# K and V slabs of a decode attention on two DMA queues instead of one

## The chip, the cores and the metric

One core of one Trainium2 chip. The metric is the device time of one execution in microseconds (us); lower is better. The core has five engines: TensorE (PE, matrix products; its weight loads are PEld in the profile), VectorE (DVE), ScalarE (ACT), GpSimd (POOL) and SyncE (SP), which in this kernel only issues DMA transfers. Transfers run on 16 DMA engines that the queues of SP and ACT share.

## The reference

Two independent problems A and B, each one decode step of attention with a sliding window: 2 batches, 1 query row of 576 numbers, 32 query heads, 16 key/value heads of 128, and the last W = 4096 of 16384 cached positions. All in bf16.

```
q = (x @ wq)                                  # x [2,1,576], wq [576,4096]
k, v = k_cache[:, :, Sk-W:], v_cache[:, :, Sk-W:]   # each key/value head serves 2 query heads
p = softmax(q k^T * 128**-0.5)                # 4096 positions
out = (p v).reshape(2, 1, 4096) @ wo          # wo [4096,576]
return concatenate([out_A, out_B], axis=-1)   # [2,1,1152]
```

## The kernel before

**Pairs and slabs.** A "pair" is one batch and one key/value head of one problem: 32 pairs in A, 32 in B, NP = 64 in all, eight to a group G. Each pair needs one K slab and one V slab of 1 MB (128 partitions x 8 KB, 32 positions of 128 numbers in each partition). With wq (4.7 MB) and wo (4.7 MB) of both problems, 153 MB come in.

**Steps.** The program is written as a list of steps t (loop from line 662 on), each in four quarters q. An engine runs its instructions strictly in the order in which the loop adds them. In step t:

- X(t): VectorE transposes K slab t into `xt`, one instruction a quarter (line 679, 4 per slab; `xt` has 3 buffers). It waits for the slab's DMA.
- S(t-1): TensorE computes the scores of pair t-1 (line 700, 8 matmuls), into one PSUM bank for each group.
- PV(t-11): TensorE multiplies the weights of pair t-11 with its V slab (line 765, 8 matmuls; for the last seven pairs line 723, 32 small matmuls in four quarters). It waits for the slab's DMA. LAG = 11 is there because the softmax of a group needs all its eight pairs.
- For pairs up to 56, ScalarE (even pairs, line 780) or VectorE (odd, line 783) copies the result out of PSUM ("eviction"), and one step later TensorE adds it up with four small matmuls (line 743, "combine").
- Every second step: a normalization on VectorE (line 555), a clear (line 565) and the projection with `wo` on TensorE (line 582).
- After the eighth pair of a group, from step 8G+8 to 8G+10, its softmax: maximum (line 377), transposes and small matmuls on TensorE (lines 381, 406, 431, 451), bias copy and exponential on ScalarE (lines 419, 427), transposes and gather on VectorE (lines 473, 487).

So step t uses K slab t and V slab t-11. After the last K slab there are eleven steps that use V alone.

**The queue.** All slabs are loaded by SP, in one order (`stream`, lines 224 to 230): K0 ... K10, K11, V0, K12, V1, ... K63, V52, V53 ... V63. Slab number s of this list goes to slot s % 9 of `ring` (NR = 9 slots), and its DMA is issued when the last reader of slab s-9 is done: the fourth transpose for a K slab, the last PV matmul for a V slab (lines 249 to 273). The last slab, V63, is loaded in four quarters, each with a semaphore of its own. The weights stand in the same list, ahead of a K slab (`w_at`, lines 231 to 237, and `ensure_stream_until`, lines 298 to 309):

- wq of A, five transfers, before K0; wq of B, one transfer before each of K13 to K17.
- wo of group G before K slab min(63, 8G+6). From G = 2 on, its issue waits (line 291) until the last projection of group G-2 has freed the buffer, which comes in step 8G+4. SP issues in order, so what stands behind it waits too.

The issues of slabs are line 272 (line 264 for V63), of wq lines 281 and 282, of wo line 294. ScalarE issues only the two small loads of x at the start (line 220).

Of the kernel before, what the change touches and what calls it, by code (L numbers as in the profile page):

```python
# [58 lines left out]

def build_kernel(nc, probs, out, cfg=None):  # L60
    cfg = dict(cfg or {})
    NR = cfg.get("NR", 9)
    NKT = cfg.get("NKT", 3)
    NTB = cfg.get("NTB", 2)
    NZQ = 2
# [1 line left out]
    LAG = cfg.get("LAG", 11)  # L67
# [21 lines left out]
    NP = PP * NPROB  # L89
# [18 lines left out]
    def is_a(i):  # L108
        return i < NP - NB_TAIL
# [12 lines left out]
    with es:  # L122
        block = es.enter_context(nc.Block())
        sb = lambda name, shape, dt: es.enter_context(nc.sbuf_tensor(name, shape, dt))
        ring = sb("ring", [128, NR, SLABW], BF16)
# [37 lines left out]
        ring_sem = [sem("ring%d" % r) for r in range(NR)]  # L163
# [4 lines left out]
        lastq_sem = [sem("lastq%d" % q_) for q_ in range(4)]  # L168
# [4 lines left out]
        def dma_op(eng, sem_h, n_dmas, fn, deps, tag):  # L173
            op = S.add(eng, fn, deps, tag)
            dma_count[sem_h] = dma_count.get(sem_h, 0) + 16 * n_dmas
            op.dma = (sem_h, dma_count[sem_h])
            return op
# [43 lines left out]
            return last  # L221
        x_dma = dma_op("act", x_sem, NPROB, f_x, [], "xload")

        stream = []
        for t in range(NP + LAG):
            if t < NP:
                stream.append(("K", t))
            if t >= LAG:
                stream.append(("V", t - LAG))
        slab_idx = {key: s for s, key in enumerate(stream)}  # L230
        w_at = {}
        for P in range(NPROB):
            t0 = 0 if P == 0 else WQ_AT + 8 * GPP * (P - 1)
# [5 lines left out]
        slab_dma = {}  # L239
        slab_quarters = {}  # L240
        slab_last_reader = {}
# [4 lines left out]
        proj = {}  # L246
        next_stream = [0]

        def issue_slab(s):
            kind, i = stream[s]  # L250
            P, g, b = pair_info(i)
            src_t = probs[P][1] if kind == "K" else probs[P][2]
            src = src_t[b, g, Sk - W:Sk, :].rearrange("(p j) d -> p (j d)", p=128)
            r = s % NR
            deps = []
            if s >= NR:
                assert slab_last_reader.get(s - NR) is not None, ("ring too small / order", s)
                deps = [slab_last_reader[s - NR]]

            if s == len(stream) - 1 and kind == "V" and not is_a(i):  # L260
                qops = []
                for q_ in range(NQ):
                    def fq(e, r=r, src=src, q_=q_):
                        return e.dma_start(ring[:, r, q_ * TQ * 128:(q_ + 1) * TQ * 128],
                                           src[:, q_ * TQ * 128:(q_ + 1) * TQ * 128]).then_inc(lastq_sem[q_], 16)
                    qops.append(dma_op("sp", lastq_sem[q_], 1, fq, deps, "%s%d_q%d" % (kind, i, q_)))
                slab_dma[s] = qops[-1]
                slab_quarters[s] = qops
                return

            def f(e, r=r, src=src):
                return e.dma_start(ring[:, r, :], src).then_inc(ring_sem[r], 16)  # L272
            slab_dma[s] = dma_op("sp", ring_sem[r], 1, f, deps, "%s%d" % (kind, i))

        def issue_wq(P, ch):
            wqP = probs[P][3]
# [21 lines left out]
        def ensure_stream_until(s_needed):  # L298
            while next_stream[0] <= s_needed:
                s = next_stream[0]  # L300
                kind, i = stream[s]
                if kind == "K":
                    for wk, a_, b_ in w_at.get(i, []):
                        if wk == "wq":
                            issue_wq(a_, b_)
                        else:
                            issue_wo(a_)
                issue_slab(s)
                next_stream[0] += 1

        tbn = [0]
# [349 lines left out]

        NT = NP + LAG + 3
        for t in range(NT):
            for q in range(NQ):
                for fn in pe_pre.get((t, q), []):
                    fn()
# [2 lines left out]
                for fn in da_pre.get((t, q + 0.5), []):  # L669
                    fn()  # L670
                if t < NP:
                    sK = slab_idx[("K", t)]
                    ensure_stream_until(sK)
                    r = sK % NR
                    c = t % NKT
                    deps = [slab_dma[sK]]
                    if t >= NKT:
                        deps.append(Sop[(t - NKT, 2 * (q // 2) + 1)])
                    xop = S.add("dve", lambda e, r=r, c=c, q=q: e.transpose(  # L679
                        xt[:, c, q * 1024:(q + 1) * 1024].bitcast(FP32), ring[:, r, q * 1024:(q + 1) * 1024].bitcast(FP32)),  # L680
                        deps, "X_%d_%d" % (t, q))
                    EVop[(t, q)] = xop
                    if q == NQ - 1:
                        slab_last_reader[sK] = xop
                i = t - 1
                if 0 <= i < NP:
                    G = group_of(i)
# [16 lines left out]
                    deps = [EVop[(i, 2 * jh_)], EVop[(i, 2 * jh_ + 1)], qev[G], st_zero[G]]  # L704
                    Sop[(i, q)] = S.add("pe", fS, deps, "S_%d_%d" % (i, q))
                i = t - LAG
                if 0 <= i < NP and not is_a(i):
                    sV = slab_idx[("V", i)]
                    ensure_stream_until(sV)
                    r = sV % NR  # L710
                    G = group_of(i)
                    pr = G % NPT
                    pl = i % 8
                    k = i // 2
                    x = k % 2
                    P, g, b = pair_info(i)

                    def fPVb(e, r=r, pr=pr, pl=pl, x=x, b=b, q=q):
                        last = None
                        for jj in range(TQ):  # L720
                            j = q * TQ + jj
                            col = tile_cols(j) + 2 * pl
                            last = e.matmul(OT[x][:, b * 64:b * 64 + NS], ring[:, r, j * 128:(j + 1) * 128],  # L723
                                            pT[:, pr, col:col + NS], start=False, stop=True, skip_group_check=True)
                        return last
                    deps = [slab_quarters[sV][q] if sV in slab_quarters else slab_dma[sV], chain[(G, "pT")], ot_zero[k], ot_last_da[x]]
                    op = S.add("pe", fPVb, deps, "PVb_%d_%d" % (i, q))
                    PVop[(i, q)] = op
                    ot_last_pe[x] = op
                    if q == NQ - 1:  # L730
                        slab_last_reader[sV] = op
                if q == NQ - 1:
                    i = t - LAG - 1
                    if 0 <= i < NP and is_a(i):
# [11 lines left out]
                        deps = acc_ev[i] + [ot_zero[k], ot_last_da[x], p_ident_b]  # L746
# [3 lines left out]
                        ot_last_pe[x] = op  # L750
                    i = t - LAG
                    if 0 <= i < NP and is_a(i):
                        sV = slab_idx[("V", i)]
                        ensure_stream_until(sV)
                        r = sV % NR
                        G = group_of(i)
                        pr = G % NPT

                        def fPV(e, r=r, pr=pr, pl=i % 8, i=i):
                            last = None  # L760
                            n_ = 0
                            for cb in range(4):
                                for jh in range(2):
                                    j0_ = 16 * jh + 4 * cb
                                    last = e.matmul(ACC[i % 2][0:8, 0:512], pC[:, pr, jh, pl, 8 * cb:8 * cb + 8],  # L765
                                                    ring[:, r, j0_ * 128:(j0_ + 4) * 128],
                                                    start=(n_ == 0), stop=(n_ == 7))
                                    n_ += 1
                            return last
                        deps = [slab_dma[sV], chain[(G, "pC")]]  # L770
                        if i >= 2:
                            deps += acc_ev[i - 2]
                        op = S.add("pe", fPV, deps, "PV_%d" % i)
                        PVop[(i, 0)] = op
                        slab_last_reader[sV] = op
                        d = [op]
                        if i >= 2:
                            d.append(comb[i - 2])
                        if i % 2 == 0:
                            ev_ = S.add("act", lambda e, i=i: e.activation(acc_sb[0:8, i % 2, :], ACC[i % 2][0:8, :], ACTF.Copy),  # L780
                                        d, "accev_%d" % i)
                        else:
                            ev_ = S.add("dve", lambda e, i=i: e.tensor_copy(acc_sb[0:8, i % 2, :], ACC[i % 2][0:8, :]),  # L783
                                        d, "accev_%d" % i)
                        evs = [ev_]
                        acc_ev[i] = evs

                for fn in da_post.get((t, q), []):
                    fn()
# [99 lines left out]
```

## Time and profile before

| what | us |
|---|---|
| median of 3 runs | 377.95 (376.51 to 378.59) |
| the profiled execution's own time | 378.42 |
| its span in the profile | 376.6 |
| TensorE busy | 296.3 (79%) |
| VectorE busy | 211.7 (56%) |
| ScalarE busy | 36.9 (10%) |
| X, one transpose (line 679) | 0.673, 256 times |
| S, one matmul (line 700) | 0.391, 512 times |
| PV, one matmul (line 765) | 0.397, 456 times |
| a slab, median from issue to landing | 19 to 20 |

The span is what the profiler saw from the first to the last instruction; the execution's own time is 1.8 us longer. "L679" in a profile line is line 679 of the code. In lists of groups and in timelines, a bracket at the end of a line tells how long the engine stood idle before it and what ended that. "SPq" and "ACTq" are the issues of DMA on those engines. A line of waits reads: engine and line, what it waited for, us in total, how many times, the longest.

### The profile page before, as it was taken

Reading aid. Unit: us, or ns where it says so; the run is one execution under the profiler, and the core shown is the slowest. Engines: PE = TensorE matmul, PEld = TensorE weight load, DVE = VectorE, ACT = ScalarE, POOL = GpSimd, SP = SyncE. Lnnn points to the kernel's source line nnn. Section 1 sums busy time; section 2 is a strip of 40 time slices with the busy share of each in tenths; the row PEclk is TensorE's granted clock in tenths of the full one; section 3 lists DMA queues with packets and bytes.
Section 4 is the critical chain, followed back from the end, with each engine's and each line's share of the span. In section 5 each row is a group of like instructions: output and inputs, shape, how many; then the busy total and the mean of one; then the engine's idle time right before and its main releaser. Section 6 shows DMA issues by size and latency. Waiting matters only on the chain.

```text
span 376.6 us, 4709 instructions
## 1 busy us (share of the span) xinstructions
PE 296.3 (79%) x1960; PEld 118.6 (31%) x1960; DVE 211.7 (56%) x429; ACT 36.9 (10%) x105; POOL 6.7 (2%) x22
## 2 busy tenths in 40 slices
PE   0397778375898989969897789868799689959786
PEld 0243223122334433313332233323333233313245
DVE  3196894235664567626864567636773467633311
ACT  1101101000101010100101010100101001000100
POOL 7000000000000000000000000000000000000000
PEclk9999989799999999989999899999999899998899
DMA  8999999999999999999999999999999999999991
GB/s 310 425 421 412 419 419 411 422 420 422 422 416 417 418 420 420 410 421 421 423 419 411 422 419 422 410 422 421 422 422 410 420 425 419 413 421 418 425 411 70
DMA packets 28661, 153.41 MB, mean 407 GB/s; under 512 B 2392, under 2 KB 10592, under 8 KB 11360
## 3 DMA queue, kind: packets, MB, share of 16 engines
q1 hardware_dynamic: 28632, 153.11, 98.9%
q8 instruction: 15, 0.25, 0.3%
q14 instruction: 6, 0.05, 0.0%
q10 hardware_dynamic: 8, 0.00, 0.0%
HBM read 153.10 MB, written 0.00 MB: 407 GB/s over the span
## 4 chain that ended last, share of the span: by engine, by line
DMA 44%; PE 33%; DVE 10%; SPq 9%; issue 1%; ACT 1%
DMA ring<-in_B_v_cache_dram 17%; DMA ring<-in_A_v_cache_dram 15%; PE acc L765 15%; PE st L700 11%; DMA ring<-in_A_k_cache_dram 8%; SPq L272 7%; DMA ring<-in_B_k_cache_dram 5%; DVE xt L679 4%; PE ot L582 3%; DVE acc_sb L783 2%; PE ot L723 2%; PE ot L743 1%; ACT pR L427 1%; DVE m L377 1%; DVE pT L473 1%
## 5 line engine op out<-in xcount | busy, mean ns | idle before, releaser
L679 DVE STREAM_TRANSPOSE xt<-ring 128x512 f32<-128x512 f32 x256 | 159.3, 673 | 66.0 <-DMA ring<-in_A_k_cache_dram 38.5
L765 PE MATMUL acc<-ring,pC 128*8 128x512 bf16 x456 | 114.7, 397 | 38.1 <-DMA ring<-in_A_v_cache_dram 22.9
L700 PE MATMUL st<-xt,zq 128*128 128x512 bf16 x512 | 134.7, 391 | 4.9 <-DVE xt L679 4.5
L700 PEld LDWEIGHTS st<-xt,zq 128*128 128x128 bf16 x512 | 42.7, 98 | 74.1 <-issue 28.5
L765 PEld LDWEIGHTS acc<-ring,pC 128*8 128x8 bf16 x456 | 36.0, 89 | 91.1 <-DMA ring<-in_A_v_cache_dram 24.5
L783 DVE CAST acc_sb<-acc 8x512 bf16<-8x512 f32 x28 | 19.0, 679 | 66.8 <-PE acc L765 66.8
L780 ACT ACTIVATE acc_sb<-acc 8x512 bf16<-8x512 f32 x29 | 17.0, 586 | 186.1 <-PE acc L765 186.1
L582 PE MATMUL ot<-wob,oTn 128*2 128x288 bf16 x128 | 20.8, 285 | 3.5 <-DVE ot L565 3.2
L743 PEld LDWEIGHTS ot<-ident_b,acc_sb 8*128 8x128 bf16 x228 | 9.2, 92 | 24.1 <-issue 16.1
L743 PE MATMUL ot<-ident_b,acc_sb 8*128 8x56 bf16 x228 | 15.6, 185 | 0.8 <-DVE acc_sb L783 0.8
L509 PE MATMUL tb<-xT,wqb 128*128 128x56 bf16 x256 | 10.2, 192 | 6.4 <-DMA wqr<-in_A_wq_dram 6.4
L582 PEld LDWEIGHTS ot<-wob,oTn 128*2 128x2 bf16 x128 | 8.0, 82 | 15.5 <-issue 8.1
L509 PEld LDWEIGHTS tb<-xT,wqb 128*128 128x128 bf16 x256 | 9.8, 99 | 7.9 <-DMA wqr<-in_A_wq_dram 6.5
L381 PE MATMUL tb<-ident_f,m 128*1 128x128 f32 x8 | 2.2, 270 | 11.7 <-DVE m L377 11.7
L555 DVE TENSOR_TENSOR oTn<-ot,rsb 128x4 bf16<-128x4 f32 x32 | 4.1, 127 | 11.2 <-PE ot L723 7.4
L541 ACT ACTIVATE zq<-tb 32x64 bf16<-32x64 f32 x32 | 7.1, 221 | 31.9 <-PE tb L523 31.6
L509 PE MATMUL tb<-xT,wqr 128*128 128x56 bf16 x64 | 9.5, 192 | 0.0
L473 DVE STREAM_TRANSPOSE pT<-pR 128x512 bf16<-128x512 bf16 x8 | 5.7, 711 | 4.6 <-ACT pR L427 4.6
L419 ACT ACTIVATE bias_sb<-tb 128x1 f32<-128x1 f32 x8 | 1.4, 171 | 61.0 <-PE tb L406 61.0
L723 PE MATMUL ot<-pT,ring 128*128 128x56 bf16 x224 | 7.0, 187 | 0.4 <-issue 0.4
L723 PEld LDWEIGHTS ot<-pT,ring 128*128 128x128 bf16 x224 | 6.2, 96 | 2.0 <-issue 1.9
L565 DVE MEMSET ot<- 128x128 f32 x30 | 5.0, 165 | 3.1
(50 smaller groups left out, 71.9 us busy)
## 6 DMA issues: line engine op xcount, KB each, us to landing
ring<-in_A_k_cache_dram SPq DMA_DIRECT2D x32, 1024.0 KB, 20.2
ring<-in_A_v_cache_dram SPq DMA_DIRECT2D x32, 1024.0 KB, 19.8
ring<-in_B_k_cache_dram SPq DMA_DIRECT2D x32, 1024.0 KB, 20.3
ring<-in_B_v_cache_dram SPq DMA_DIRECT2D x31, 1024.0 KB, 19.3
wob<-in_A_wo_dram SPq DMA_DIRECT2D x4, 1152.0 KB, 18.4
wob<-in_B_wo_dram SPq DMA_DIRECT2D x4, 1152.0 KB, 9.5
wqb<-in_A_wq_dram SPq DMA_DIRECT2D x4, 1024.0 KB, 8.0
wqb<-in_B_wq_dram SPq DMA_DIRECT2D x4, 1024.0 KB, 21.9
```

The costliest lines, as they stand in the source:

```text
L272: return e.dma_start(ring[:, r, :], src).then_inc(ring_sem[r], 16)
L473: chain[(G, "pT")] = S.add("dve", lambda e: e.transpose(pT[:, pr, 0:PW], pR[:, G % 2, :]), deps, "cTpx_%d" % G)
L509: last = e.matmul(bank[:, hl * 64:hl * 64 + NS], w_, x_, start=(ch == 0), stop=(ch == NCH - 1))
L541: last = e.activation(dst, src, ACTF.Copy)
L582: last = e.matmul(OT[half][0:Bb, ACC0:ACC0 + NH], oTn[:, orr, h, :], wob[:, pc, hsl + h, half * NH:(half + 1) * NH], start=False, stop=Tru ...
L679: xop = S.add("dve", lambda e, r=r, c=c, q=q: e.transpose(xt[:, c, q * 1024:(q + 1) * 1024].bitcast(FP32), ring[:, r, q * 1024:(q + 1) * 1 ...
L700: last = e.matmul(ST[x][:, 0:512], zq[:, p4, zr, pl, 16 - 16 * jh:144 - 16 * jh], mv, start=False, stop=True, skip_group_check=True)
L723: last = e.matmul(OT[x][:, b * 64:b * 64 + NS], ring[:, r, j * 128:(j + 1) * 128], pT[:, pr, col:col + NS], start=False, stop=True, skip_g ...
L743: last = e.matmul(OT[x][:, b * 64:b * 64 + NS], acc_sb[0:8, i % 2, 128 * jl4:128 * jl4 + 128], ident_b[0:8, 2 * jl4:2 * jl4 + NS], start=F ...
L765: last = e.matmul(ACC[i % 2][0:8, 0:512], pC[:, pr, jh, pl, 8 * cb:8 * cb + 8], ring[:, r, j0_ * 128:(j0_ + 4) * 128], start=(n_ == 0), st ...
L780: ev_ = S.add("act", lambda e, i=i: e.activation(acc_sb[0:8, i % 2, :], ACC[i % 2][0:8, :], ACTF.Copy), d, "accev_%d" % i)
L783: ev_ = S.add("dve", lambda e, i=i: e.tensor_copy(acc_sb[0:8, i % 2, :], ACC[i % 2][0:8, :]), d, "accev_%d" % i)
```

## The change

The nine slots are divided: 4 for SP's queue, 5 for ScalarE's.

- SP's list is now K0 to K63 with the weights ahead of them as before, and at its end V56, V58, V60 and V62. Entry n goes to slot n % 4 and waits for the last reader of entry n-4.
- The other 60 V slabs (V0 to V55, V57, V59, V61, V63) are issued by ScalarE, in this order, into five slots of their own. The issue of V slab number n of this list is added to ScalarE's instructions right behind the point where the last reader of number n-5 was added (for pairs with an eviction, behind the eviction), and waits for that reader. The first five, V0 to V4, are issued after the last transpose of K6 to K10.
- V63 is still loaded in four quarters, now by ScalarE.

Nothing else changes: the steps, the order of all other instructions and the bytes that are moved are the same. The core of the diff:

```
-    NR = cfg.get("NR", 9)
+    NRK = cfg.get("NRK", 4)
+    NRV = cfg.get("NRV", 5)
+    NR = NRK + NRV
...
-        stream = []
-        for t in range(NP + LAG):
-            if t < NP:
-                stream.append(("K", t))
-            if t >= LAG:
-                stream.append(("V", t - LAG))
-        slab_idx = {key: s for s, key in enumerate(stream)}
+        V_LATE = NP - 8
+        sp_v = [i for i in range(V_LATE, NP) if i % 2 == 0]
+        act_v = [i for i in range(NP) if i not in sp_v]
+        stream = [("K", t) for t in range(NP)] + [("V", i) for i in sp_v]
+        k_slot = {key: n % NRK for n, key in enumerate(stream)}
+        v_slot = {("V", i): NRK + n % NRV for n, i in enumerate(act_v)}
+        slot_of = dict(k_slot)
+        slot_of.update(v_slot)
...
-        def issue_slab(s):
-            kind, i = stream[s]
+        def issue_slab(eng, key, deps):
+            kind, i = key
...
-            slab_dma[s] = dma_op("sp", ring_sem[r], 1, f, deps, "%s%d" % (kind, i))
+            slab_dma[key] = dma_op(eng, ring_sem[r], 1, f, deps, "%s%d" % (kind, i))
+
+        next_act = [0]
+
+        def act_issue_after(op_key, op):
+            n = next_act[0]
+            if n >= len(act_v):
+                return
+            want = ("K", LAG - NRV + n) if n < NRV else ("V", act_v[n - NRV])
+            if op_key == want:
+                issue_slab("act", ("V", act_v[n]), [op])
+                next_act[0] += 1
...
-                issue_slab(s)
+                issue_slab("sp", stream[s], [slab_last_reader[stream[s - NRK]]] if s >= NRK else [])
...
         for t in range(NT):
+            if t == NP:
+                ensure_stream_until(len(stream) - 1)
...
                     if q == NQ - 1:
                         slab_last_reader[sK] = xop
+                        act_issue_after(sK, xop)
...
                     if q == NQ - 1:
                         slab_last_reader[sV] = op
+                        act_issue_after(sV, op)
...
                         acc_ev[i] = evs
+                        act_issue_after(sV, op)
```

More of the change, by code (lines that the diff above doesn't have):

```diff
@@ L253, in issue_slab @@
             src = src_t[b, g, Sk - W:Sk, :].rearrange("(p j) d -> p (j d)", p=128)
[L254 to L260, printed above, removed]
+            r = slot_of[key]
+            if key == ("V", NP - 1):
                 qops = []
@@ L265, in fq @@
                                            src[:, q_ * TQ * 128:(q_ + 1) * TQ * 128]).then_inc(lastq_sem[q_], 16)
-                    qops.append(dma_op("sp", lastq_sem[q_], 1, fq, deps, "%s%d_q%d" % (kind, i, q_)))
-                slab_dma[s] = qops[-1]
-                slab_quarters[s] = qops
+                    qops.append(dma_op(eng, lastq_sem[q_], 1, fq, deps, "%s%d_q%d" % (kind, i, q_)))
+                slab_dma[key] = qops[-1]
+                slab_quarters[key] = qops
                 return
@@ L671, in build_kernel @@
                 if t < NP:
-                    sK = slab_idx[("K", t)]
-                    ensure_stream_until(sK)
-                    r = sK % NR
+                    sK = ("K", t)
+                    ensure_stream_until(t)
+                    r = slot_of[sK]
                     c = t % NKT
@@ L707, in build_kernel @@
                 if 0 <= i < NP and not is_a(i):
-                    sV = slab_idx[("V", i)]
-                    ensure_stream_until(sV)
-                    r = sV % NR
+                    sV = ("V", i)
+                    r = slot_of[sV]
                     G = group_of(i)
@@ L752, in build_kernel @@
                     if 0 <= i < NP and is_a(i):
-                        sV = slab_idx[("V", i)]
-                        ensure_stream_until(sV)
-                        r = sV % NR
+                        sV = ("V", i)
+                        r = slot_of[sV]
                         G = group_of(i)
```

## The prediction

> **What bounds the kernel now.** I read the page first, then the waits, then the timeline of the start and of the last 40 us. The page's slices show the DMA engines full in all slices but the last, and one queue carries nearly all of it:
>
> ```profile
> DMA  8999999999999999999999999999999999999991
> GB/s 310 425 421 412 419 419 411 422 420 422 422 416 417 418 420 420 410 421 421 423 419 411 422 419 422 410 422 421 422 422 410 420 425 419 413 421 418 425 411 70
> q1 hardware_dynamic: 28632, 153.11, 98.9%
> ```
>
> So the stream of 153.1 MB is the limit, not an engine. The completions in the trace, transfer by transfer, say how even it is: K63 lands at 340.98 us, V61 ten slabs later at 365.81, so one 1 MB slab costs **2.483 us**. A change of queues removes no byte. What it can change is whether the engines ever run dry, their rate, and **the order** in which slabs arrive.
>
> Order matters only where compute cannot absorb it, so the next view is TensorE's timeline at the end (start, us, line, form):
>
> ```profile
> 338.54 2.40 PE L765 MATMUL acc<-ring,pC 128*8 128x512 bf16 x8 [3.32 <-DMA ring<-in_B_v_cache_dram]
> 340.87 3.03 PE L700 MATMUL st<-xt,zq 128*128 128x512 bf16 x8
> ...
> 344.04 1.89 PE L765 MATMUL acc<-ring,pC 128*8 128x512 bf16 x8
> ...
> 346.98 1.48 PE L700 MATMUL st<-xt,zq 128*128 128x512 bf16 x6
> 348.39 0.28 PE L743 MATMUL ot<-ident_b,acc_sb 8*128 8x56 bf16 x4
> 348.60 1.89 PE L765 MATMUL acc<-ring,pC 128*8 128x512 bf16 x8
> 351.86 0.27 PE L381 MATMUL tb<-ident_f,m 128*1 128x128 f32 x1 [1.37 <-DVE m L377]
> ...
> 372.02 1.62 PE L723 MATMUL ot<-pT,ring 128*128 128x56 bf16 x56
> 373.89 0.65 PE L582 MATMUL ot<-wob,oTn 128*2 128x288 bf16 x4 [0.25 <-DVE oTn L555]
> ```
>
> The row at 338.54 is PV 51, which waited for V51 (landed 338.49). It is the last wait of TensorE for a slab. From 348.60 (PV 53) on there is only compute: the last group's softmax, PV 54 to 63, the projections, the output. PV 53 ends at 350.49 and the span at 376.6: a **tail of 26.1 us** that no DMA shortens, though V63's last quarter lands only at 371.60. That tail starts when the scores of pair 63 are done, that is after K63. So the time is set by when K63 (and V51) land, not by when the last byte does. K63's transpose in this run:
>
> ```profile
> 340.97 0.68 DVE L783 CAST acc_sb<-acc 8x512 bf16<-8x512 f32 x1 [2.46 <-PE acc L765]
> 341.58 2.47 DVE L679 STREAM_TRANSPOSE xt<-ring 128x512 f32<-128x512 f32 x4
> ```
>
> It ends at 344.05; TensorE takes up S 63 at 345.86. K63 has about 1.8 us to spare, and the wait behind it (S 63 done 348.46) another 2.
>
> **The change, part by part.**
>
> *Issue of V on ScalarE (added: 60 slabs, of them V63 in four pieces; removed from SP: the same).* A slab's issue takes 0.33 us on SP when the queue has room (median row of L272 for V). 60 of them are 20 us on an engine that is 10% busy. Each stands behind the PV that frees its slot, right after that pair's eviction. What is queued behind it on ScalarE is evictions of later pairs, the exponentials and bias copies, which TensorE feeds after that PV anyway. V63's four issues (4 x 0.43 us) stand ahead of the last `rsb` copy, which is needed by the norm of pairs 56/57, some 7 us later in the trace. Cost: 0; if a full queue held ScalarE as it held SP behind the second `wo`, up to 17.65 us for one issue, with K traffic flowing meanwhile:
>
> ```profile
> 42.10 2.92 SPq L294 DMA_DIRECT2D wob<-in_A_wo_dram  x1
> 45.06 17.65 SPq L272 DMA_DIRECT2D ring<-in_A_k_cache_dram  x1
> ```
>
> *SP's waits.* The waits of the queue:
>
> ```profile
> SPq L272 <- DVE xt L679: 91.1, 28, 17.5
> SPq L294 <- PE ot L582: 62.0, 6, 10.9
> ```
>
> The second is the load of `wo`, which waits for an old projection and stops K and V behind it, 10.9 us at worst. V no longer waits there. It buys nothing, since the engines stay full through those waits.
>
> *Four K slots at the start.* Only K flows then. Transfers in order: wq to 14.5 us, K0 17.0, K1 19.5, K2 22.0, K3 24.5. K4 is issued when the transpose of K0 ends (17.03 + 2.49 = 19.5), K5 when that of K1 does: three memsets come between (to 21.1), so 23.5. An issue reaches the engines in some 1.5 us (0.8 us issue, first packet 1.8 on this trace, and the 0.44 of the issue itself), so K5 is ready at 25.4 and K4 flows until 26.9: 1.5 us of cover, the tightest place. Next come wo0 and K6 to 36.2; the transpose of K6 ends at 38.7, when K8 and K9 (to 43.8) are still to come, and V0 is issued then. Nothing runs dry: cost 0; without the cover, up to 2.5 us.
>
> *The rate with two queues.* No trace here has two loaded queues. Bounds from the rows: the mean from 100 to 300 us is 418.5 GB/s, the best stretch (360 to 364) 426, 1.8% more; the worst slices with `wo` 410, 2% less. Over 350 us that is -6.3 to +7 us. An 8 KB packet takes 309 ns and a slab of 8 per engine 2.483 us, so one queue leaves no gap to fill. I take 0.
>
> *The order, where the change acts.* In the old order K63 has V0 to V51 ahead of it: 52 slabs. In the new one V runs in its own queue with five slots: V n goes out as soon as PV n-5 is done, whether it is due or not. K shares its queue with all weights, 4.7 MB of problem B's wq between K12 and K17 and 1.2 MB of wo every eight pairs. So K becomes the late one and V's slots fill: each step TensorE waits for K, one V goes out and lands within the step. Replaying the start with slabs in turn, K14 lands with V0 to V8 in (14 - 6); in the old order it would be V0 to V2. It stays so, since each step consumes one of both and only K's queue carries more. At the end, V57 goes out after PV 51 and lands about with K63; V59 goes out after PV 52, just as K63 lands. V56, V58, V60 and V62 stand behind K63 on SP. So at K63's landing 57 V slabs are in (V0 to V55 and V57), **five more than before**: 5 x 2.483 = 12.4 us, K63 at 353.4.
>
> From there: transpose 2.49, its second half's scores 0.93 (half of the 1.85 us row), 0.2 for the combine, PV 53 1.83: ends at 353.4 + 5.45 = 358.85 instead of 350.49, **+8.4 us**. The 4 us of slack of the old tail are in this. Then the same 26.1 us: the span is 385.0. V63 goes out after PV 54 (about 365.5) with the queues still full, and lands near 371; TensorE needs it near 381. So alternating the last eight V saves nothing that is late.
>
> The profiled execution took 378.42 us (span 376.6 and 1.8 around it); with +8.4 it is 386.8. The median of the runs, 377.95, lies 0.5 below it, so I predict **386.4 us**. Each slab more or less of V ahead of K63 moves it by 2.5 us: four give 383.9, three 381.4, six 388.9.
>
> **Who gets the turn.** How two queues share is seen here once only: a 2.2 KB load of x on ScalarE's queue, issued beside the first wq slab.
>
> ```profile
> 1.38 0.24 ACTq L220 DMA_DIRECT2D x_sb<-in_B_x_dram  x1
> 6.04 1.59 DVE L347 COPY x_dup<-x_sb 2x128 bf16<-2x128 bf16 x2 [3.01 <-DMA x_sb<-in_B_x_dram]
> ```
>
> Its packets ran at 4.99 and 5.43 us by the trace, the other x load's at 1.72: it waited for a whole slab's share, then had its turn. That is what the replay uses: turns of one slab. The Trainium skill, "DMA: Bandwidth & Descriptors", section "Queues, rings and completion order", has each engine go round the queues it has work for, a packet of some 9 to 17 descriptors at a time; the trace agrees (eight packets of data and one completion). The same page's "Rules for kernel authors" says that spreading DMAs over issuing engines does not help bandwidth and only saves issue time; by that sentence alone the time would stay at 378.
>
> **The rivals.**
>
> *The two streams stay abreast (378, chance 0.09).* If V's lead never fills (ScalarE late with issues, or K served more), K63 lands with V52 again, at 341. V53 to V55 then alternate with V56, V58, V60, V55 landing near 356, and PV 55 ran at 358.6: no loss. For it: issues on SP after a `wo` did take up to 17.65 us, and ScalarE might be held too. Against: that comes once, at 45 us, and later ones are 0.6 to 3.3 us against a lead of five steps of 5 us.
>
> *K is served first (388 to 391, chance 0.10).* Then V is the late one: V51 lands behind K63 and three or four of V56 to V62, four or five slabs or 9.9 to 12.4 us later, and 38.1 us follow it as now. Against it: the wait of the x load, which had its turn.
>
> *The rate rises (372, chance 0.05), the other side.* If two queues interleave packets so that the 426 GB/s stretch becomes the rule, V51 lands 1.8% of 336 us, or 6.0 us, earlier, and if the streams also stay abreast the time is 372. It is faster by over 0.5% from a rise of 0.6% on. With the five slabs ahead of K63 it would take 2.9%, more than any stretch shows. Against it: the packets leave no gap now.
>
> *ScalarE or DMA lose more than I count (over 391, chance 0.06):* a queue that holds ScalarE for several us at each `wo`, or engines that run dry at the start.
>
> **How the numbers follow.** The forecast, K late by four to six slabs, has 0.70: 383.9 to 388.9. The range runs from 380 (three slabs or a slightly better rate) to 391 (K first, or a rate 1% lower); the abreast and the faster case and the longest losses, 0.20 together, lie outside. 0.5% is about what a measurement of this kernel can tell from no change; faster by more has 0.05, within it 0.09, slower 0.86.
>
> **What the new profile would show.** Right: TensorE and VectorE wait for K slabs all along and hardly for V; K63 lands near 353 with V57 in; the span ends some 31 us after K63's landing; the stream ends near 371 at 98% busy; SP still waits at L294's `wo`, ScalarE's issues take 0.3 to 0.5 us. Wrong: slices of DMA below 9 at the start (slots too few), GB/s off 420, TensorE waiting for V in the last third (K first), or K63 near 341 (abreast).

## The result, and the profile after

The changed kernel takes **392.33 us** (median of 4, 391.37 to 393.45) against 378.27 (4 runs): ratio 1.0387, 95% interval 1.0352 to 1.0423. The forecast was 386.4, in a range of 380 to 391: the sign was right, the loss is 14 us instead of 8. The profiled execution took 391.37 us, with a span of 389.5: 12.9 longer than the span before. In the experiments below, one run each of e1, e3, e4, e6 and e16 was slow (over 1.5% above the fastest of its kernel): without it their medians are 383.39, 390.37, 384.16, 384.72 and 389.09, the ratio given for e1 still contains it, and in e3, e4 and e6 it is the profiled one, so of these three only the lead, issue durations and SP's waits are used.

The profile page of the changed kernel, the lines that answer to those of before:

```profile
DMA  8999999999999999999999999999989999999930
GB/s 313 421 412 419 422 419 422 412 421 421 421 422 407 422 418 421 402 422 424 421 406 390 426 421 421 409 423 421 423 353 336 424 423 421 412 421 421 412 123 2
q1 hardware_dynamic: 19560, 90.19, 56.8%
q10 hardware_dynamic: 9080, 62.92, 39.3%
```

Two queues now carry the bytes (q10 is ScalarE's). The slices of 390 near 210 us and of 353 and 336 near 290 us are below every slice of before but its first and its last. From 280 to 300 us the DMA engines stood partly still (busy share 0.90, next section). The waits of VectorE and TensorE, first in the kernel before:

```profile
DVE xt L679 <- DMA ring<-in_A_k_cache_dram: 38.5, 9, 9.4
DVE xt L679 <- DMA ring<-in_B_k_cache_dram: 27.2, 12, 5.1
```

```profile
PE acc L765 <- DMA ring<-in_A_v_cache_dram: 22.9, 12, 5.9
PE acc L765 <- DMA ring<-in_B_v_cache_dram: 15.1, 11, 3.4
```

and in the changed kernel:

```profile
DVE xt L691 <- DMA ring<-in_A_k_cache_dram: 65.5, 14, 12.6
DVE xt L691 <- DMA ring<-in_B_k_cache_dram: 44.2, 13, 10.8
```

```profile
PE st L713 <- DVE xt L691: 46.3, 14, 8.0
```

VectorE waits 109.7 us for K (65.7 before), with single waits up to 12.6. TensorE's own list has no wait for a V slab any more, where it had 38.0 us: it waits for transposes. K is late and V early, as forecast. The end, TensorE's timeline (start, us, form):

```profile
354.49 3.60 PE L713 MATMUL st<-xt,zq 128*128 128x512 bf16 x8 [7.21 <-DVE xt L691]
...
358.31 2.68 PE L777 MATMUL acc<-ring,pC 128*8 128x512 bf16 x8
...
362.05 1.48 PE L713 MATMUL st<-xt,zq 128*128 128x512 bf16 x6
...
363.66 1.89 PE L777 MATMUL acc<-ring,pC 128*8 128x512 bf16 x8
...
386.83 0.65 PE L592 MATMUL ot<-wob,oTn 128*2 128x288 bf16 x4 [0.25 <-DVE oTn L565]
```

and VectorE's transposes of K62 and K63:

```profile
353.13 2.49 DVE L691 STREAM_TRANSPOSE xt<-ring 128x512 f32<-128x512 f32 x4 [10.84 <-DMA ring<-in_B_k_cache_dram]
...
357.17 2.49 DVE L691 STREAM_TRANSPOSE xt<-ring 128x512 f32<-128x512 f32 x4 [0.99 <-DMA ring<-in_B_k_cache_dram]
```

K62 lands at 353.10 (336.00 before), K63 at 357.14 (340.98 before). PV 53 is the row at 363.66: it ends at 365.55 instead of 350.49, and only compute follows.

**Where the 16.2 us at K63 come from.** By K63's landing 146.4 MB are in, before it was 141.4. The 5.0 MB more, at the 417.7 GB/s of the stream before, are 12.0 us: V slabs that were not due. The same 146.4 MB would have been in at 352.9 at that rate; they were in at 357.14: 4.2 us are stream time lost.

The lost time lies around two waits of SP: 15 us from 200 us on at 391 GB/s and 20 us from 280 on at 345, against 417.7, are 4.4 us. SP's waits for a projection, and its timeline around the wo of group 6:

```profile
SPq L304 <- PE ot L592: 61.4, 6, 10.6
```

```profile
266.79 16.35 SPq L271 DMA_DIRECT2D ring<-in_B_k_cache_dram  x4
293.43 0.38 SPq L304 DMA_DIRECT2D wob<-in_B_wo_dram  x1
293.86 16.44 SPq L271 DMA_DIRECT2D ring<-in_B_k_cache_dram  x5
```

The last of the four K slabs of the first row, K53, was issued at 282.81 and landed at 290.63. Until 286.63 all four K slots were taken. Then K50 had been read and K54 had a free slot, but it stands behind wo 6 and went out at 293.86. So for 2.8 us nothing of SP's queue was under way, and of ScalarE's queue one or two V slabs: each waits for the PV that frees its slot (V44 went out at 288.44, V45 at 292.32). At wo 4 SP's queue was empty from 203.55 to 204.68.

### The profile page after: what moved, and what is told of

Read it like the earlier page. It is cut to its first block, busy times and chain, and to the rows that moved or that the text cites. A ratio compares the mean times of both kernels' runs of the same rounds, so it can differ in the third digit from the quotient of the medians.

```text
span 389.5 us, 4708 instructions
## 1 busy us (share of the span) xinstructions
PE 303.4 (78%) x1960; PEld 120.1 (31%) x1960; DVE 209.7 (54%) x429; ACT 36.9 (9%) x105; POOL 6.9 (2%) x22
## 4 chain that ended last, share of the span: by engine, by line
DMA 48%; DVE 23%; PE 23%; SPq 2%; issue 2%; ACT 1%
DMA ring<-in_A_k_cache_dram 25%; DMA ring<-in_B_k_cache_dram 23%; DVE xt L691 16%; PE st L713 9%; PE acc L777 8%; PE ot L592 3%; DVE acc_sb L795 2%; PE ot L735 1%; SPq L271 1%; ACT pR L437 1%; DVE pT L483 1%; DVE m L387 1%; PE ot L756 1%; DVE ot L575 1%; SPq L291 1%
## 5 line engine op out<-in xcount | busy, mean ns | idle before, releaser
L713 PE MATMUL st<-xt,zq 128*128 128x512 bf16 x512 | 145.6, 415 | 47.1 <-DVE xt L691 46.3
L777 PE MATMUL acc<-ring,pC 128*8 128x512 bf16 x456 | 110.7, 387 | 0.0
L713 PEld LDWEIGHTS st<-xt,zq 128*128 128x128 bf16 x512 | 44.4, 102 | 121.6 <-DVE xt L691 61.8
## 6 DMA issues: line engine op xcount, KB each, us to landing
wob<-in_A_wo_dram SPq DMA_DIRECT2D x4, 1152.0 KB, 10.7
```

Of the source, the lines that this page charges most:

```text
L713: last = e.matmul(ST[x][:, 0:512], zq[:, p4, zr, pl, 16 - 16 * jh:144 - 16 * jh], mv, start=False, stop=True, skip_group_check=True)
```

## The experiments

Times are medians, ratios against the kernel before on the same chip with 95% intervals. "V lead" is how many V slabs more are in than the kernel before has at that point (V0 to V51 when K63 lands), "rate" the bytes in by K63's landing over the time from 2.4 us; both are counted from the completions in the trace of the profiled execution.

| run | us | ratio | K63 lands | V lead there | rate, GB/s |
|---|---|---|---|---|---|
| before | 378.27 | 1 | 340.98 | 0 | 417.7 |
| changed | 392.33 | 1.0387 | 357.14 | 4 | 412.8 |
| e1 third wo buffer | 383.91 | 1.0211 (1.0126 to 1.0296) | 349.72 | 3 | 417.1 |
| e2 shared slots, two queues | 394.82 | 1.0469 (1.0415 to 1.0524) | 358.92 | 6 | 411.8 |
| e3 all V on ScalarE | 392.41 | 1.0366 (1.0289 to 1.0443) | | 4 | |
| e4 six K, three V slots | 385.31 | 1.0167 (1.0090 to 1.0244) | | 1 | |
| e5 as e1, one queue | 379.79 | 1.0051 (1.0027 to 1.0075) | 343.41 | 1 | 417.5 |
| e6 wo by ScalarE | 385.03 | 1.0157 (1.0106 to 1.0207) | | 0 | |
| e8 as e1, wo in long rows | 382.57 | 1.0116 (1.0072 to 1.0159) | 349.49 | 3 | 419.7 |
| e11 as e4, third wo buffer | 381.87 | 1.0093 (1.0060 to 1.0126) | 345.84 | 1 | 417.6 |
| e12 WO_LEAD 3 | 397.55 | 1.0548 (1.0478 to 1.0619) | 362.76 | 5 | 409.6 |
| e13 wo by GpSimd | 380.31 | 1.0072 (1.0043 to 1.0102) | 348.08 | 2 | 417.7 |
| e16 as e12, last wo late | 389.23 | 1.0256 (1.0180 to 1.0332) | 354.5 | 2 | 404.9 |

(The leads at K63 are 56 - 52 = 4 for the changed kernel, and so on.)

**e1, e2, e3, e4: which part of the change?**

e1 adds a third buffer for wo:

```
-        wob = sb("wob", [128, 2, 8, NOUT], BF16)
+        wob = sb("wob", [128, 3, 8, NOUT], BF16)
-            deps = [proj[4 * (G - 2) + 3]] if G >= 2 else []
+            deps = [proj[4 * (G - 3) + 3]] if G >= 3 else []
```

> The changed kernel with a third buffer for wo, so that no wo load waits for a projection that still lies ahead and SP's K issues are never held behind it. Theory (order, and engines that run dry at wo): the 4.3 us in which the stream stood still disappear, the slices below 400 GB/s near 200 and 285 us go, K62 lands near 349 and the time falls by 3 to 4.5 us to about 388; the rest of the loss, the V slabs ahead of K62 and K63, stays. Rival (two loaded queues share the engines badly): no change, 392.

Measured: 383.91, 8.4 us back, twice what was expected. The window 280 to 300 us, changed kernel and then e1 (the length, the busy time of PE, PEld, DVE, ACT and POOL with the number of instructions, the clock granted to TensorE, the busy share of the DMA engines, and GB/s):

```profile
280.00:300.00 20.00, 19.26 (x108) 7.30 (x106) 14.70 (x32) 2.83 (x9) 0.00 (x0) 1.00 0.90 345
```

```profile
280.00:300.00 20.00, 19.92 (x109) 7.25 (x106) 10.57 (x21) 2.06 (x6) 0.00 (x0) 1.00 1.02 416
```

No stream time is lost (417.1 GB/s), so two loaded queues do not slow the engines: the contention rival falls. The other half of the gain is 1.6 MB fewer ahead of K63.

e2 keeps nine shared slots and gives out a slab when the one nine places earlier in the due order is read, but issues V from ScalarE:

```
+        slot_of = {key: s % NR for s, key in enumerate(due)}
+        nine_back = {key: due[s - NR] for s, key in enumerate(due) if s >= NR}
...
-            want = ("K", LAG - NRV + n) if n < NRV else ("V", act_v[n - NRV])
+            want = nine_back[("V", n)]
```

> Two queues, V still issued by ScalarE, but with the nine shared slots and the rule of the kernel before: each slab goes out when the slab nine places earlier in the due order has been read. Theory (order): K63 lands near 341 with V51 or V52, no V lead builds up, 378 within 1.5 us. Rival (two loaded queues, or ScalarE as the issuing engine, cost time by themselves): 385 to 392, as the queues are as loaded as in the changed kernel.

Measured: 394.82; the expectation fell, and so did the idea that the issue rule keeps the order. The last wo, issued at 334.2, landed at 354.0, and seven V slabs (V51 to V57) landed between; K62 stood behind it and landed at 356.5, when 58 V were in. It was the single queue, first in first out, that kept K ahead of V, not the slots.

e3 is `sp_v = []`:

> The changed kernel with all 64 V slabs on ScalarE's queue (the alternation of the last eight undone). Theory: the same V slabs lie ahead of K62 and K63 and the tail is compute, so the time stays within 1 us of 392; the last byte may land later than 376 us without effect. Rival (the out-of-order last V slabs are what delays the end): 2 to 5 us faster.

Measured: 392.41, with runs from 389.65 to 396.30: no effect of the alternation of the last eight V is seen, though one of 2 us could hide in that spread. The lead at K63 is that of the changed kernel.

e4 is `NRK` 6 and `NRV` 3:

> The changed kernel with six K slots and three V slots. Theory: V can be at most two to three slabs ahead of its use instead of four to five, so K62 and K63 land 2 slabs (5 us) earlier, and six K slots cover the wo wait (4.3 us back): 383 to 385. If three slots are too few for V, which takes 9.7 us from issue to landing in the changed kernel, TensorE waits for V and it ends at 386 to 395. Rival (two queues cost by themselves): 392.

Measured: 385.31. V's lead is down to 1, but SP now waits 131.6 us for projections (61.4 in the changed kernel): no number of K slots lets a K pass a wo that waits ahead of it in the list. That part of the expectation was wrong, and the time lies just above its 383 to 385.

**e5, e6, e8, e11: turns, slots, or wo?**

e5 has e1's slots and buffers, with every transfer on SP's queue at the point where its slot comes free:

```
-                issue_slab("act", ("V", act_v[n]), [op])
+                issue_slab("sp", ("V", act_v[n]), [op])
...
                         slab_last_reader[sK] = xop
+                        ensure_stream_until(min(t + NRK, NP - 1))
```

> The slots and waits of the changed kernel (4 K, 5 V, three wo buffers as in e1, all 64 V) with every transfer issued by SP on one queue, each entry at the point where its slot comes free. Theory now (the queue's first-in first-out kept the due order; two queues that take turns let V run ahead whenever SP's queue carries weights): K63 has 52 or 53 V ahead of it, lands within 3 us of 341, and the time is 378 to 381, faster than e1's 383.9. Rival (the split into 4 and 5 slots makes the order): as e1, 383 to 385, with 55 V in at K63's landing.

Measured: 379.79, as the theory had it: 4.1 us faster than e1 with the same slots (every run of e5 lies below every run of e1). The split costs 1.8 us, the second queue 4.1 on top, the changed kernel's two wo buffers 8.4 on top of that.

e6 issues wo of groups 2 to 7 from ScalarE, behind the projection:

```
             proj[k] = S.add("pe", f, deps, "proj_%d" % k)
+            if k % 4 == 3 and k // 4 + 2 < NG:
+                issue_wo(k // 4 + 2, "act")
```

> The changed kernel with the six waiting wo loads issued by ScalarE, right behind the projection that they wait for (two wo buffers, as in the changed kernel). SP never waits for a projection, and the weights stand in V's queue instead of K's. Theory: no lost stream time, and V falls back a little at each wo instead of K; K62 and K63 land 8 to 14 us earlier than in the changed kernel (341 to 347): 378 to 383. Rival (third buffer in e1 helped for another reason; turns with small rows hurt whichever queue they are in): 388 to 392.

Measured: 385.03, between the two, and K63 has no V ahead that is not due. What the wo now holds up is ScalarE, e6's timeline:

```profile
248.49 12.94 ACTq L271 DMA_DIRECT2D ring<-in_B_v_cache_dram  x1
261.48 0.22 ACT L551 ACTIVATE zq<-tb 32x64 bf16<-32x64 f32 x1 [15.59 <-issue]
```

A V slab issued 3 us behind a wo held ScalarE for 12.94 us, and its evictions with it. How much of the 7 us over the kernel before this explains is not shown.

e8 is e1 with wo in rows eight times as long, 128 for a wo instead of 1024 (the rows reach the wrong heads):

```
-                                   woP[...].rearrange("(h d) n -> d h n", d=128))
+                                   woP[...].rearrange("(d h) n -> d h n", d=128))
```

> e1 with wo read in rows of 9216 bytes instead of 1152 (the same bytes, but the rows of wo reach the wrong heads, so the projection is not the reference's). Theory of the turns: a queue's turn is a few descriptors whatever they hold, so in e1 one wo gives V three slabs and itself 10 to 14 us; with long rows it takes about the time of one slab and one V slab, 5 to 7 us, fewer V are ahead of K63 (53 or 54 instead of 55) and the time falls by 2 to 5 us to 379 to 382. Without the theory: only what short rows cost by themselves, 0.23 us each in the kernel before, 2 us in all: 382.

Measured: 382.57, near the 382 of the alternative and not clear of e1 (the intervals overlap); K63 still has 55 V. From the landing of the transfer ahead of it to its own, a wo of group 2 to 7 takes 5.3 us with 1.1 MB of V landing beside it, where e1 has 8.0 to 10.1 us and 1.9 to 2.5 MB (3.0 us in the kernel before, alone). So the theory had the time of a wo right: short rows do let more V pass. But V's lead at K63 and the total time hardly hang on that.

e11 is e4 with e1's third buffer.

> e4 (six K slots, three V slots, two queues) with the third wo buffer of e1, so that SP never waits for a projection. Theory: what is left of the loss in e1 is the V slabs that are ahead of K63 beyond their due place (55 in instead of 52); three slots allow one or two (53), K63 lands 2 to 5 us earlier than in e1 (345 to 348) with the stream at 417 GB/s: 379 to 382. Rival (two queues cost something besides the order): 383 to 385, as e1.

Measured: 381.87 (378.23 to 383.34): in the range. In the profiled execution, one of the fastest of its ten at 378.53, K63 has one V too many instead of three and lands 3.9 us earlier than in e1's.

**e12, e15, e14, e13, e16: the wait for wo, or wo itself?** e12 moves wo two K slabs later in the list (`WO_LEAD` 3), so that SP need not wait.

> The changed kernel with one constant changed: WO_LEAD 3 instead of 5, so each wo stands two K slabs later in SP's list (ahead of K 8G+8; group 7 ahead of K63), where the projection that it waits for is already done or nearly so. Two wo buffers as before. Theory (SP's wait ahead of the wo is what lost 8 us): the same gain as the third buffer of e1, 382 to 386, and few us of waiting on line 304. Rival (the third buffer helped in another way): 390 to 392.

Measured: 397.55, slower than the changed kernel, though SP's waits for wo did go:

```profile
SPq L304 <- PE ot L592: 13.4, 6, 5.7
```

So SP's wait is not the only way to lose stream time: here the waits went and more of it is lost (409.6 GB/s). What the trace shows in e12 is a wait for a K slab behind wo and then a rush. K48 was issued at 252.2, right behind wo, and landed at 277.6. The windows 270 to 280 and 280 to 296:

```profile
270.00:280.00 10.00, 0.55 (x3) 0.04 (x1) 2.37 (x4) 0.00 (x0) 0.00 (x0) 0.72 1.01 422
280.00:296.00 16.00, 13.93 (x67) 5.42 (x68) 11.58 (x26) 1.72 (x5) 0.00 (x0) 0.86 0.90 358
```

For 10 us TensorE does 0.55 us of work and the engines run full: they bring wo, and V into its free slots (lead 5). Then all K slots fill too, TensorE (13.93 of 16 us) is the bound, no slot is free to issue into, and the stream drops to 358 GB/s: at 286 us, K52 alone is under way, and no V. In the changed kernel it is the same from 282 us until a K slot comes free at 286.63; from there to 293.86 it is SP's wait for wo 6 that keeps K54 back.

e15 and e14 leave out the loads of wo for groups 2 to 7, in the kernel before and in the changed one (`if G >= 2: wo_dma[G] = wo_dma[G % 2]`).

> The kernel before without the loads of wo for groups 2 to 7: their projections use the two wo blocks already in the buffers, so the output is not the reference's. 7.1 MB less: the reference for e14. All theories: the stream is 6 x 2.8 to 3.0 us shorter, 360 to 362.

> The changed kernel without the loads of wo for groups 2 to 7 (the same wrong projections as e15). Theory 1 (wo in the K queue is what makes K wait 9 to 15 us while V fills its slots): without it K and V alternate, no stream time is lost, and what is left is the lead of 2 or 3 V slabs that problem B's wq sets up: 4 to 7 us over e15, 364 to 368. Theory 2 (two queues lose it by themselves, wo or not): 12 to 14 us over e15, 373 to 376.

Measured: 358.87 and 362.44 (ratios to the kernel before 0.9503, 0.9474 to 0.9531, and 0.9600, 0.9561 to 0.9639). Without wo the change costs 3.6 us, not 14; K63 has one V too many, and the rate is 418.6 GB/s. So some 10 of the 14 us need wo.

e13 takes wo out of SP's queue: GpSimd issues it on a third queue, each behind its projection.

```
-            wo_dma[G] = dma_op("sp", wo_sem[pc], 1, f, deps, "wo%d" % G)
+            wo_dma[G] = dma_op("pool", wo_sem[pc], 1, f, deps, "wo%d" % G)
```

> The changed kernel with all wo loads issued by GpSimd on a third queue, each right behind the projection that it waits for (two buffers; the first two behind the transposes of K2 and K10). Theory 1: SP's queue holds K alone, the long waits for K go, no stream time is lost, V's lead stays at 2 or 3: 381 to 385, about as e1. Theory 2 (the place of wo does not matter): 390 to 394.

Measured: 380.31, the lowest median of the kernels that load K and V on two queues, and better than expected: the loads wait for the same projections, but no K stands behind them. VectorE's longest wait for a K slab of B is 3.9 us instead of 10.8:

```profile
DVE xt L691 <- DMA ring<-in_B_k_cache_dram: 50.7, 25, 3.9
```

GpSimd's wo moves in packets of 4608 bytes instead of 1152, so e13 changes that besides the queue; e8, where long rows alone gave about 1 us, speaks for the queue.

e16 is e12 with the wo of group 7 ahead of V56.

> e12 (WO_LEAD 3) with the wo of group 7 ahead of V56 in SP's list instead of ahead of K63. Theory 1: in e12 the last such wait, 12 us between X 62 and X 63, fell right at the tail; without it K63 lands some 5 us behind K62 (353): 387 to 390, and the stream time lost at the other wo stays lost. If that place is all that was wrong with e12: 382 to 386.

Measured: 389.23 (385.37 to 393.64), 8.3 less than e12. K63 lands 8.3 us earlier, with 5.0 MB less ahead of it and without the wait of 12 us between X 62 and X 63. The lost stream time does not shrink: 10.7 us by K63 (404.9 GB/s), against 7.0 in e12.

**e7, e9, e10: towards a faster kernel.** If the end is set by K63 and V51, what stands ahead of them and is not due should go behind. e7 is the kernel before with the wo of group 7 ahead of V56 in the list; e9 and e10 add LAG 12 and 13.

```
+                if kind == "V" and i == NP - 8:
+                    issue_wo(NG - 1)
                 issue_slab(s)
```

> The kernel before with one edit: the last wo (group 7) is loaded ahead of V56 instead of ahead of K62. Theory of the tail (the end is compute that starts with V51 and K63, the bytes behind them are free): V51, K62 and K63 land 2.9 us earlier, and the time falls by 2 to 3 us to 375 to 376. Rival (the last byte sets the end): no change, 378.

> The kernel of e7 (one queue, wo of group 7 ahead of V56) with LAG 12 instead of 11: every V slab stands one step later in the due order, so K63 has V0 to V50 ahead of it instead of V0 to V51. Theory of the tail (it starts with K63): K63 lands 2.5 us earlier (335.5); one more PV has to follow it, partly hidden in the waits of the last softmax: 1 to 2.5 us faster than e7, 374 to 375.5. Rival (TensorE's work behind V50 just grows by what K63 gains): 376 to 377, no change.

> As e9 with LAG 13: K63 5 us earlier than in e7 (333). Theory of the tail: 1 to 4 us faster than e7 if the added PV hide in the last softmax, 373 to 375.5; since only about 2 us of that softmax is idle on TensorE, most of the gain should be gone by LAG 13. If the last bytes (V63 near 371) become the end: 375 to 376.

Measured: 376.59 (0.9984, 0.9962 to 1.0006), 376.52 (0.9971, 0.9954 to 0.9988) and 376.61 (0.9966, 0.9950 to 0.9982). K63 lands 3.0, 5.7 and 8.1 us earlier and the profiled span shrinks by 1.8, 1.9 and 2.2: there the gain ends, short of all three expected ranges. TensorE waits for V at the end, e9's timeline:

```profile
368.76 0.38 PE L726 MATMUL ot<-pT,ring 128*128 128x56 bf16 x8 [1.07 <-DMA ring<-in_B_v_cache_dram]
...
371.33 0.38 PE L726 MATMUL ot<-pT,ring 128*128 128x56 bf16 x8 [0.25 <-DMA ring<-in_B_v_cache_dram]
```

The last bytes (371.29) set the end now. They do so in e7 already, where TensorE waits 1.48 us for V at 368.88 and the last byte lands at 371.38: the kernel before was only some 2 us from that bound. e9 and e10 beat both kernels, by 0.3%; e7's interval reaches 1.

## Why the prediction was wrong

**What held.** The bound, the direction, and the main term. In e1, e2, e5, e8, e11, e12, e13 and e16 the span grew by 0.9 to 4.7 us less than K63 was late, so the end does follow K63, with a slack like the 4 us of the prediction. Five slabs ahead of K63 were forecast as 12.4 us, and 5.0 MB, 12.0 us, were there (four whole V slabs and parts of V56 and V57, which were in flight). The rate with two queues is what was taken: 417.1 and 417.7 GB/s in e1 and e13 against 417.7. The sentence of the Trainium skill on spreading DMAs over issuing engines ("DMA: Bandwidth & Descriptors", "Rules for kernel authors") agrees on bandwidth; that the time stays the same does not follow from it, since the order changes. On ScalarE's issues the forecast was right as well: no V issue took over 0.37 us before the last slab, not even while SP was held.

**The step that failed: the price of 0 for SP's wait at wo.** The prediction said of the loads of wo that leaving V out of their wait "buys nothing, since the engines stay full through those waits", and of the four slots "Nothing runs dry". That held at the start (421 GB/s in the second slice), but not later. In the kernel before, SP stopped for as long (62.0 us in all), but slabs were issued 19 to 20 us before they landed; in the changed kernel these are 15 us for K and under 10 for V. There K 22, 30, 38, 46, 54 and 62 each went out 7.2 us after their slot had been read, and at wo 4 and wo 6 SP's queue ran empty. 4.2 us of stream time were lost by K63. The third wo buffer takes SP's wait away, and with it the loss (e1, 417.1 GB/s). In e12 stream time is lost with little of that wait, so the wait is what cost it in the changed kernel, and not the only thing that can.

**The sum, term by term.** K63 landed at 357.14 instead of 353.4: the 4.2 us, less 0.4 for the bytes. From there to the end of PV 53 the sum has 5.45 us and the run 8.41, because TensorE, after its wait of 7.21 us, still had S 62 (3.60 us) and PV 52 (2.68) to do. The tail behind it took 24.0 instead of 26.1, PV 54 alone 1.89 instead of 3.36. Together that is the 4.5 us between a span of 385.0 and 389.5. The remaining 1.4 of the 5.9 us between 386.4 and 392.33 is chance: the forecast took the median 0.5 below the profiled execution, as it was before, and in the changed kernel it lies 1.0 above.

**The reason behind the main term was too smooth, and its size partly luck.** The prediction had V's lead as a steady state ("It stays so, since each step consumes one of both"). Its replay had the queues take turns of one slab; they alternate in single rows (last section), so a wo took 8.0 to 10.1 us beside V in e1, where alone it took 3.0. And the completions show a cycle. In the changed kernel the lead is 5 slabs when K14 lands, falls to 2 by K21, jumps to 4 at K22, right behind wo 2, falls to between 1 and 3 again, and so on at each wo; at K61 it is 2. K63 met a lead of 4 because wo 7 stands just ahead of K62. Without wo the lead at K63 is 1 (e14), with wo on a queue of its own a steady 2 (e13), and in one queue the same slots keep it at 1 (e5). Take wo out of the program and the change costs 3.6 us (e14, e15); out of K's queue, 2.4 over the kernel before (e13).

**The chain of costs,** each from medians: split slots in one queue +1.8 (e5), second queue +4.1 (e1), and from the third wo buffer to two +8.4 (+3.6 and +8.9 with e1 at 383.39). It is a chain of kernels, not a sum of separate causes: e12 has hardly any of SP's wait and is slower still.

**What stays open:** why e1, with waits for K of 8.5 to 11.2 us at three of its wo loads, loses no stream time, and e12, with waits of 12, loses 7.0. One difference stands in the timelines: in e12 the late slab is K48, and on VectorE the maximum of a softmax stands behind its transpose (280.61 us), so the weights that PV needs come late too; in e1 the late slab is K54. No run separates that. And the profiled executions are one each: e11's runs spread over 5 us, so its place among e1 and e13 is not settled to a microsecond.

## What to carry to other kernels

When one stream is the bound and its consumer takes two kinds of data in step, the first-in first-out order of a single queue is itself the schedule. Here a second queue moved no byte faster, and let the side that had nothing else in its queue run ahead. Before splitting a queue, find what else stands in it (weights behind a wait, transfers of another kind): with that on a queue of its own the loss fell from 14 to 2.4 us here, though it did not become a gain. And read the end from the last transfer that the compute tail waits for, not from the last byte.

## What the runs showed of the hardware

In these traces a held issue stopped only the engine that made it. In the changed kernel SP stood 15.73 us on the issue of a K slab behind a wo, and ScalarE's issues went through meanwhile. SP's timeline, then ScalarE's:

```profile
52.53 15.73 SPq L271 DMA_DIRECT2D ring<-in_A_k_cache_dram  x1
```

```profile
52.53 0.36 ACTq L271 DMA_DIRECT2D ring<-in_A_v_cache_dram  x1
...
65.55 0.34 ACTq L271 DMA_DIRECT2D ring<-in_A_v_cache_dram  x1
```

Behind a wo of its own queue ScalarE was held like SP, 12.94 us in e6.

The two queues take turns row by row, not slab by slab as the prediction's replay had it. The packets' records show it where the end of one packet fits the start of just one other within 6 ns, which puts the two on the same DMA engine: in e1 from 100 to 340 us, an 8 KB row of V was followed by a packet of SP's queue 3334 times and by another V row 156 times. In e13 the three queues follow one another in the same way. So where they alternate, each row of wo (1152 bytes) lets an 8 KB row of V pass. In e8 a wo has 8 rows for each DMA engine, as a slab has, and one V slab (1.1 MB) lands beside it; in e1 it has 64, and 1.9 to 2.5 MB of V landed. That is less than row for row, which would be eight slabs: a row of wo was followed by another one 900 times and by V's queue 702 times, and why V's queue was passed over then is not shown. The Trainium skill ("DMA: Bandwidth & Descriptors", "Queues, rings and completion order") has a turn of 9 to 17 descriptors; these records show turns of one.
